# A float32 attention and mixer kernel: token transposes in halves, mixing products in pairs, loads on another queue, and five reorderings around them

## The chip, the cores and the metric

The kernel runs on one core of a Trainium2 chip. The metric is the device time of one execution in microseconds; lower is better.

## The reference

Inputs are `q`, `k`, `v` of 4 batches x 8 heads x 576 positions x 64, a small network `w1`, `b1`, `w2` (hidden width 32) that makes a position bias, and the mixer's weights, which are float64.

```python
scores = q @ k.T / 8
x = log1p(|i - j|) / log1p(max(i, 1))              # 576 x 576
bias = relu(x[..., None] @ w1 + b1) @ w2           # one 576 x 576 table per head
out = softmax(scores + bias) @ v                   # per batch and head
x = out, heads side by side                        # 4 x 576 x 512
u = x + transpose(transpose(x) @ U @ V)            # mixing over positions, U 576 x 32
result = u + relu(u @ w_ch1) @ w_ch2               # 512 -> 2048 -> 512
```

## The kernel before

It has four stretches.

**The network** (0 to 68 us) makes the bias of all heads in 36 tables. For each table one hidden block comes from ScalarE and three from VectorE (`bias_hid`, lines 308 and 310), TensorE multiplies them (`bias_mm`, line 317), ScalarE brings the result into one of eight `ring` slots (`bias_out`, line 332), and two DMAs on SyncE's queue (four for each of the first four tables, line 342) carry it into its place in the bias (line 338). The ten hidden slots let VectorE run about two tables ahead. Meanwhile the first pair of heads does a part of its work (`first(...)`: `Sn` is a scores block on TensorE, `Tn` adds the bias on VectorE, `En` is the exponential on ScalarE). Six DMAs, `pair_loads(1)`, fetch pair 1's q and k; they are issued at tables 9 to 14 of the loop.

Every DMA of the program counts its completion on one of eight semaphores, which are taken in turn in program order over all the queues. An issue on any queue waits until the transfer that had its semaphore before, eight DMAs earlier in program order, has landed.

**Attention** (76 to 300 us) runs over 16 pairs of heads, 9 slots each, in an order written out by hand (`SLOTS`: engines take their instructions in this order; one prime is the pair before, two primes the one before that). `R0` and `PM` divide the rows left over from 4 x 128 (`norm_m`, line 417, on GpSimd) and `I0` transposes them; `X` are other transposes, `AV` the product with v, `A` and `D` bring the output back into token order in `x_sb`. `Q1` to `Q4` split the next pair's q and k into a high and a low float32r part on GpSimd. From pair 2 on the float64 weights of group 0 are converted beside (`VA`, `VD`, `VS`, `VJ`: ScalarE, VectorE, GpSimd).

**Mixing** comes once for each batch, three times in the pair behind a batch and once at the end: `MT` to `MX` build the product with U, `H0` to `H4` multiply by V, one 128-row block each (`mix_h`), `HD` adds x (`mix_add`, line 594), `U` stores to DRAM (`mix_store`).

**The channel network** (from about 290 us) takes 18 blocks of 128 tokens: `make_ut` transposes a block (line 717), splits it into high and low parts, `mlp1` (line 756) and `mlp2` (line 779) multiply. It runs 36 steps, 4 groups of weights by 9 blocks of 256 tokens. The weights of group 1 are converted while steps 3 to 8 run: `background(n)` takes the next n small groups of conversion instructions after each part of a step. All PSUM tiles share four buffers; a new tile takes the buffer that was released longest ago.

Of the kernel before, what the change touches and what calls it, by code (L numbers as in the profile page):

```python
# [20 lines left out]
DM = H * D  # L21
# [4 lines left out]
P = 128  # L26
# [15 lines left out]
CW = 256  # L42

SLOTS = (
    "S0 E7' X10' MF' AV1'' T0 E8' MS' N8'' I1' VS1' C10' MX' E0 CO1'' M' VJ1' CI1' N0 CM' H3' "
    "VP0' R0",
    "S1 HD3' U3' T1 VA0",
    "S2 T2 X20' H4' Q1 VP1' Q2 C20' HD4' U4' LA",
    "S3 T3 PM H1' H0' X30' Q3",
    "S4 C30' HD1' U1' H2' HD0' U0' E3 T4 E2 HD2' U2' R8''",  # L50
    "S5",
    "S6 VD0 T5 E1 A0'' AV0' E4 VS0 A1'' VA1 T6 Q4 LB D0'' VJ0 I0 X00 D1'' CO0' CI0 E6",
    "S7 MT VD1 C00",
# [12 lines left out]
def kernel(  # L66
# [75 lines left out]
    qk_ops, raws = {}, {}  # L142
    v_t = {}

    def pair_loads(p):

        b, hp = divmod(p, HP)

        src = qk[b, hp]

        def part(i, lo, to, n):
            if (p, i) not in raws:
                raws[p, i] = rawp.tile([P, (QQ, KA + KB)[i]], F32, tag=f"raw{i}", name="raw")
            return raws[p, i][lo : lo + D, to : to + n]

        def q(lo):
            nc.sync.dma_start(
                out=part(0, lo, 0, QQ).rearrange("d (t n) -> d t n", t=2),
                in_=src[:, 0 : 2 * (S + LEFT)].rearrange("d (t n) -> d t n", t=2)[:, :, 0:S],
            )  # L160

        def k(lo, to, n, a):
            nc.sync.dma_start(out=part(1, lo, to, n), in_=src[:, a : a + n])

        return [
            lambda: q(0),
            lambda: q(D),
            lambda: k(0, 0, KA, K0),
            lambda: k(D, 0, KA, K0 + KA),
            lambda: k(0, KA, KB, K0 + S),  # L170
            lambda: k(D, KA, KB, 2 * K0 - KB),
        ]
# [10 lines left out]
    def prep_ops(p, early=False):  # L183


        hi = qkp.tile([P, 2 * KD * TB], F32R, tag="hi", name="hi")
        lo = qkp.tile([P, QKW], F32R, tag="lo", name="lo")
        qk_ops[p] = (hi, lo)

        parts = [(raws[p, 0], hi[:, 0:QQ], lo[:, 0:QQ]), (raws[p, 1], hi[:, QQ:QKW], lo[:, QQ:QKW])]  # L190

        def high(raw, h, l):
            nc.gpsimd.tensor_scalar(out=h, in0=raw, scalar1=1.0, scalar2=0.0, op0=ALU.mult, op1=ALU.add)

        def low(raw, h, l):
            eng = nc.vector if early else nc.gpsimd
            eng.tensor_tensor(out=l, in0=raw, in1=h.bitcast(F32), op=ALU.subtract)  # L197

        return [lambda o=o, i=i: o(*parts[i]) for i in range(2) for o in (high, low)]

# [337 lines left out]
            )  # L538

    mixt = {}  # L540
    stages = cycle([(tabp, "tab"), (tabp, "extra"), (mix, "y"), (mix, "th"), (mix, "tl")])

    def mix_t():
        t = psum("mt")[:, 0, :]
# [18 lines left out]
        mixt["t"] = t  # L563

    def mix_hi():
        mixt["h"] = mix.tile([P, DM], F32R, tag="th", name="th")
        nc.scalar.copy(out=mixt["h"], in_=mixt["t"])

    def mix_lo():
        mixt["l"] = mix.tile([P, DM], F32R, tag="tl", name="tl")  # L570
        nc.vector.tensor_tensor(out=mixt["l"], in0=mixt["t"], in1=mixt["h"].bitcast(F32), op=ALU.subtract)

    def mix_fold():
# [9 lines left out]
        o = mixt["q"][D:P]  # L583
        nc.vector.tensor_tensor(out=o, in0=mixt["s"][D:P], in1=o.bitcast(F32), op=ALU.subtract)

    def mix_h(c):
        mixt[c] = psum("mh")[:, 0, :]
        mm(mixt[c], lhsT=vq[:, c * P : (c + 1) * P], rhs=mixt["q"], start=True, stop=True)  # L588

    def mix_add(c):  # L590
        n = P if c < 4 else LEFT
        pool, tag = next(stages)
        y = mixt["y", c] = pool.tile([P, DM], F32, tag=tag, name="y")
        nc.vector.tensor_tensor(out=y[0:n], in0=mixt[c][0:n], in1=x_sb[0:n, c, :], op=ALU.add)

    def mix_store(b, c):
        n = P if c < 4 else LEFT
        nc.sync.dma_start(out=u_dram[b * S + c * P : b * S + c * P + n, :], in_=mixt["y", c][0:n])

    NP = B * HP  # L600

# [110 lines left out]
        nc.sync.dma_start(out=acc[i], in_=u_dram[i * P : (i + 1) * P, :])  # L712

    def make_ut(j, i):
        bank = psum("tu")[:, 0, :].rearrange("p (k q) -> p k q", k=KD)
        for k in range(KD):
            nc.tensor.transpose(bank[:, k, :], acc[j * TT + i][:, k * P : (k + 1) * P], ident)  # L717
        sl = slice(i * P, (i + 1) * P)
        nc.scalar.copy(out=uth[j][:, :, sl], in_=bank)  # L719
        if j == SPLIT:  # L720
            parts = [(at[:, :, i, :], k, k + n) for at, k, n in utl[j]]
        else:
            parts = [(utl[j][:, :, sl], 0, KD)]
        for dst, a, e in parts:
            nc.vector.tensor_tensor(  # L725
                out=dst, in0=bank[:, a:e], in1=uth[j][:, a:e, sl].bitcast(F32), op=ALU.subtract
            )

    def split(g, which, k, a, e):
        def fin(y):  # L730
            h, l = (w[k][:, a:e] for w in wq[g][2 * which : 2 * which + 2])
            nc.scalar.copy(out=h, in_=y)
            nc.gpsimd.tensor_tensor(out=l, in0=y, in1=h.bitcast(F32), op=ALU.subtract)

        return fin
# [140 lines left out]
    order = [32, 33, 34, 35] + [8 * c + i for c in range(4) for i in (0, 4, 1, 5, 2, 6, 3, 7)]  # L876
    early = {11: 0, 19: 1, 21: 2, 28: 3, 30: 4, 36: 5, 37: 6}
    preps[-1] = prep_ops(0, True)
    second = pair_loads(1)
    for i in range(len(order) + 3):  # L880
        if i == 2:
            nc.vector.tensor_scalar(
                out=table[:, CUT:NTAB], in0=table[:, CUT:NTAB], scalar1=w1_sb, scalar2=None, op0=ALU.mult
            )
        if 2 <= i < len(order) + 2:
            bias_mm(order[i - 2])
        if i < len(order):
            bias_hid(order[i])
        if i == 1:
            nc.vector.reciprocal(out=g8_sb, in_=ps)  # L890
        if 2 <= i < len(order) + 2:
            bias_out(order[i - 2])
        if i == 22:
            preps[0] = prep_ops(1, True)
        if 5 <= i < 9 or i in (22, 23, 25, 26):
            preps[-1 if i < 9 else 0].pop(0)()
        if 9 <= i < 15:
            second.pop(0)()
        if i - 1 in early:
            first(f"E{early[i - 1]}")  # L900
        if i - 1 == 11:
            first("N0")
        if i in early:
            first(f"S{early[i]}", f"T{early[i]}")
    done.update((f"Q{i}", 0) for i in range(1, 5))
    constants()
    x_sb = mix.tile([P, 5, DM], F32, tag="x_sb", name="x_sb")
    vq = mix.tile([P, 640], F32R, tag="vq", name="vq")
    nc.gpsimd.memset(x_sb[D:P, 4, :], 0.0)

    jobs = [(u32, 160, fin_u)]
    jobs += [(v4[:, a : min(a + CW, 640)], min(CW, 640 - a), fin_v(a, min(a + CW, 640))) for a in range(0, 640, CW)]
# [21 lines left out]
    for p in range(NP):  # L934
        if p > 0:
            new_pair(p)
        for s in range(9):
            if s == 3:
                load_v(p)
            if p == CONV_FROM - 1 and s in (0, 2, 4):  # L940
                conv["jobs"][s // 2][0]()
            period(p, s)
            if p == NP - 3 and s == 1:
                wq[0] = early_weights(0)
                feed = chain(first_weights(0), first_weights(1))
            if p == NP - 2 and s == 1:
                wq[0] += early_weights(1)
            if p == NP - 1 and s == 1:
                for i in range(9):
                    acc[i] = bias3[:, i * DM : (i + 1) * DM]  # L950
            if (p, s) in FEED:
                next(feed, None)
            if p == NP - 1 and s in (1, 2, 3):
                load_acc(2 * s - 2)
                load_acc(2 * s - 1)

    def run(*steps):
        for o in steps:
            o()

    m = [mlp1(n) for n in range(3)]
    y = [mlp2(n) for n in range(2)]
    def last_mix(c):
        mix_h(c)
        mix_add(c)
        mix_store(B - 1, c)

    def ut_in(t):
        return t[:, LINE : LINE + UT].rearrange("p (k f) -> p k f", k=KD)
# [38 lines left out]
    mix_fold()  # L1008
    mix_sum()
    mix_rest()  # L1010
    for i, c in enumerate((4, 0, 1, 2, 3)):
        run((m[2][1:] + y[1])[i])
        last_mix(c)
        if i > 2:
            make_ut(3, i - 3)
    p1.close()

    def pool(name, bufs):
# [13 lines left out]
    for n in range(2, NG * NB + 1):  # L1032
        g, j = divmod(n, NB)
        if n == 2:
            t = w3p.tile([P, LINE + 4 * WQ - 2 * DM], F32R, tag="w", name="wq")
            w = [t[:, LINE + i * DM : LINE + (i + 1) * DM] for i in range(4 * KD - 2)] + spare
            wq[1] = [w[i : i + KD] for i in range(0, 4 * KD, KD)]
        elif j == 0 and g + 1 < NG:
            wq[g + 1] = wq[g - 1]
        if g + 1 < NG and (n == 2 or (j == 0 and g > 0)):  # L1040
            queue += pipeline(weight_jobs(g + 1, split))
            queue[1:1] = [[]] * (8 if n > 2 else 0)
        steps = mlp1(n) if 2 < n < NG * NB else []
        if 2 < n < NB - 1:
            feed = [lambda i=i: make_ut(n + 1, i) for i in range(TT)]
            steps = steps + feed if n == 3 else feed + steps
        if n > 2:
            steps += mlp2(n - 1)
        for i, o in enumerate(steps):
            o()  # L1050
            background(2 if n >= NB or i == 0 else 1)


# [68 lines left out]
```

## Time and profile before

| | us |
|---|---|
| median of 3 runs | 725.97 (724.94 to 728.79) |
| the profiled execution | 726.99 |
| its span in the trace | 725.1 |
| TensorE busy (matmul) | 692.3, 95% of the span |
| VectorE / ScalarE / GpSimd busy | 446.5 / 354.6 / 216.8 |

The profiled execution is 1.0 us above the median. TensorE is busy in 95% of the span, so what is read below is where it is not, where it runs at its lower clock, and what it spends between matmuls.

### The profile page before, as it was taken

The page shows a single profiled execution, that of the slowest core. Times are in us where ns is not written, and L with a number is a line of the kernel's source. Part 1 is how long each engine was busy: PE and PEld are TensorE (multiplying, and loading weights), DVE is VectorE, ACT ScalarE, POOL GpSimd, SP SyncE. Part 2 cuts the span into 40 slices and gives each one's busy share as a digit, 9 for nine tenths or more (in the row PEclk, how much of TensorE's full clock was granted, in tenths as well). Part 3 has the DMA queues.
Part 4 walks back from the last instruction along what each step waited for, and adds up shares of the span by engine and source line. Part 5 has one row for each costly group of instructions (what it writes and reads, how often), then busy time and mean ns, then how long its engine had stood idle before and what let it go on. Part 6 is the DMA issues. An engine that isn't in the chain of part 4 may idle for free.

```text
span 725.1 us, 16712 instructions
## 1 busy us (share of the span) xinstructions
PE 692.3 (95%) x6708; PEld 575.9 (79%) x6708; DVE 446.5 (62%) x929; ACT 354.6 (49%) x763; POOL 216.8 (30%) x234
## 2 busy tenths in 40 slices
PE   6987799999999999999799999999999999999998
PEld 4554677667767867868689899898898998988986
DVE  7997589999999886434567548812288522122122
ACT  6887699879989889511444233410135201101000
POOL 1000457755755744100243325600056300000000
PEclk9999799999999999999899999999999999999999
DMA  4767734564565365104321212300022000010111
GB/s 127 185 197 215 186 84 110 143 200 141 154 178 172 99 179 180 44 1 148 136 71 62 59 40 77 102 15 1 1 77 96 18 1 1 1 59 31 57 54 63
DMA packets 39885, 68.25 MB, mean 94 GB/s; under 512 B 5888, under 2 KB 12544, under 8 KB 39808
## 3 DMA queue, kind: packets, MB, share of 16 engines
q1 hardware_dynamic: 39424, 67.01, 31.9%
q8 instruction: 53, 0.87, 0.5%
q14 instruction: 24, 0.20, 0.1%
q10 hardware_dynamic: 384, 0.18, 0.1%
HBM read 45.02 MB, written 11.53 MB: 78 GB/s over the span
## 4 chain that ended last, share of the span: by engine, by line
PE 85%; DVE 5%; ACT 3%; DMA 3%; issue 2%; SPq 1%; POOL 0%; DVEq 0%; ACTq 0%; POOLq 0%
PE po L779 28%; PE ph L756 27%; PE o L498 10%; PE sc L366 9%; PE tb L440 4%; PE bs L317 2%; DVE ring L310 2%; DMA bias<-ring 1%; PE mh L588 1%; ACT p L399 1%; PE tx L440 1%; PE ti L440 1%; DMA wraw<-in_w_ch_dram 1%; PE tu L717 1%; DVE wt L220 1%
## 5 line engine op out<-in xcount | busy, mean ns | idle before, releaser
L761 ACT ACTIVATE hh<-ph 128x1024 fp32r<-128x1024 f32 x36 | 36.9, 1025 | 190.5 <-PE ph L756 190.4
L762 DVE SCALAR_TENSOR_TENSOR hh<-ph,hh 128x1024 fp32r<-128x1024 f32 x36 | 44.1, 1225 | 130.6 <-ACT hh L761 130.6
L236 POOL TENSOR_TENSOR wy<-wt,wy 128x256 int32<-128x256 int32 (+1 forms) x68 | 52.5, 772 | 218.5 <-DVE wt L231 189.5
L779 PE MATMUL po<-bias,hh 128*128 128x512 f32 x432 | 105.0, 398 | 3.7 <-DVE hh L762 3.7
L399 ACT ACTIVATE p<-p,st 128x576 f32<-128x576 f32 x128 | 98.3, 772 | 3.9 <-DVE st L381 3.8
L381 DVE CUSTOM_DVE_ANT_0 p<-sc,bias 128x576 f32<-128x576 f32 x128 | 92.8, 751 | 8.7 <-PE sc L366 5.4
L779 PE MATMUL po<-wq,hh 128*128 128x512 f32 x360 | 98.1, 394 | 0.0
L779 PEld LDWEIGHTS po<-bias,hh 128*128 128x128 f32 x432 | 81.3, 192 | 20.7 <-DVE hh L762 4.2
L498 PE MATMUL o<-pt,v 128*64 128x320 f32 (+1 forms) x640 | 84.7, 411 | 0.1
L779 PEld LDWEIGHTS po<-wq,hh 128*128 128x128 f32 x360 | 66.5, 188 | 14.3
L756 PE MATMUL ph<-ut,bias 128*128 128x256 f32 x512 | 66.9, 279 | 0.3 <-DVE ut L725 0.3
L498 PEld LDWEIGHTS o<-pt,v 128*64 128x64 f32 x640 | 43.1, 136 | 28.9 <-DVE st L381 1.3
L756 PE MATMUL ph<-ut,wq 128*128 128x256 f32 x512 | 65.0, 276 | 0.0
L756 PEld LDWEIGHTS ph<-ut,bias 128*128 128x128 f32 x512 | 63.0, 188 | 1.0 <-DVE ut L725 0.5
L756 PEld LDWEIGHTS ph<-ut,wq 128*128 128x128 f32 x512 | 62.0, 188 | 1.0
L197 POOL TENSOR_TENSOR lo<-raw,hi 128x1152 fp32r<-128x1152 f32 (+1 forms) x28 | 59.4, 2122 | 1.7
L366 PE MATMUL sc<-hi 64*128 64x288 f32 (+1 forms) x320 | 56.7, 346 | 2.0 <-DVE x_sb L527 0.6
L423 ACT COPY pt<-tb 128x1024 f32<-128x1024 f32 x48 | 47.8, 1014 | 17.8 <-PE tb L440 9.4
L317 PE MATMUL bs<-ring,small_sb 128*32 128x64 f32 (+2 forms) x780 | 51.1, 355 | 5.3 <-DVE ring L310 2.4
L782 DVE TENSOR_TENSOR acc<-po,acc 128x512 f32<-128x512 f32 x36 | 24.9, 692 | 49.8 <-PE po L779 49.7
L756 PE MATMUL ph<-bias 128*128 128x256 f32 x352 | 48.5, 282 | 0.7 <-ACT bias L719 0.7
L366 PE MATMUL sc<-lo,hi 64*128 64x288 f32 (+1 forms) x320 | 48.8, 295 | 0.0
(106 smaller groups left out, 1219.8 us busy)
## 6 DMA issues: line engine op xcount, KB each, us to landing
wraw<-in_w_ch_dram SPq DMA_DIRECT2D x64, 256.0 KB
raw<-in_qk_dram SPq DMA_DIRECT2D x32, 288.0 KB
bias<-ring SPq DMA_DIRECT2D x64, 144.0 KB
v<-in_vp_dram SPq DMA_DIRECT2D x16, 320.0 KB
u_dram<-y SPq DMA_DIRECT2D x16, 256.0 KB
raw<-in_qk_dram SPq DMA_DIRECT2D x32, 88.0 KB
raw<-in_qk_dram SPq DMA_DIRECT2D x32, 72.0 KB
bias<-u_dram SPq DMA_DIRECT2D x9, 256.0 KB
```

Of the source, the lines that this page charges most:

```text
L197: eng.tensor_tensor(out=l, in0=raw, in1=h.bitcast(F32), op=ALU.subtract)
L236: nc.gpsimd.tensor_tensor(out=st["y"], in0=st["t"], in1=st["y"], op=ALU.add)
L317: mm(bs[T][32 * cg : 32 * cg + 32, a, o : o + n], lhsT=w2_sb, rhs=hids[T][cg][:, i : i + n], start=True, stop=True, tile_position=(0, 32 * ...
L366: mm(ps[0:n, a, 0:HALF], lhsT=q[r, q0 : q0 + n], rhs=k[r, k0 : k0 + HALF], start=(i == 0), stop=(i == len(terms) - 1),)
L381: nc.vector.tensor_tensor_reduce(out=halves(dst), in0=d.pop(("ps", s))[:, :, 0:HALF], in1=halves(bias_at(p % HP, s)), scale=-0.125, scalar ...
L399: nc.scalar.activation(out=dst, in_=dst, func=AF.Exp, bias=st[:, s : s + 1], scale=-1.0, accum_out=st[:, 10 + s : 11 + s])
L423: nc.scalar.copy(out=out, in_=in_)
L440: nc.tensor.transpose(bank[:, h, i * D : (i + 1) * D], src[r, a : a + P], ident[r, r])
L498: mm(o[hd * D : (hd + 1) * D, 0:n], lhsT=v[:, vb * D : (vb + 1) * D], rhs=pt[:, pb, :], start=(j == 0), stop=(j == 4),)
L756: mm(d, lhsT=w, rhs=u, start=(i == 0), stop=(i == 3 * KD - 1))
L762: nc.vector.scalar_tensor_tensor(out=hl[n], in0=st["ps"], scalar=0.0, in1=hh[n].bitcast(F32), op0=ALU.max, op1=ALU.subtract)
L779: mm(ps, lhsT=h, rhs=w, start=(m == 0), stop=(m == 3 * FG - 1))
```

## The change

1. `make_ut` transposes a block by `flip`, as attention does: for each 128 columns two transposes of 64 rows, into two banks, and the copies read both banks.
2. Mixing's five products go into three PSUM tiles (two, two, one), with one add and one store for each; the slots of `H`, `HD`, `U` are moved.
3. `pair_loads(1)` is issued on ScalarE's queue instead of SyncE's.
4. `R0` and `PM` of pair 0 stand right behind the network's loop, and the clearing of a part of `x_sb` on GpSimd, which stood ahead of them, moves to the beginning of pair 1.
5. The low part of q is made in three pieces, that of k in two (`prep_ops`, from pair 2 on).
6. The high part of group 0's second weights is copied by VectorE instead of ScalarE (`split`).
7. After the last mixing, the two `make_ut(3, .)` come ahead of the two parts of `mlp2(1)`, and mixing's products ahead of both.
8. The conversion of group 1's weights gets seven empty groups behind its first loads, and takes two groups at every fourth part of a step.

```diff
@@ SLOTS
-    "S0 E7' X10' MF' AV1'' T0 E8' MS' N8'' I1' VS1' C10' MX' E0 CO1'' M' VJ1' CI1' N0 CM' H3' "
+    "S0 E7' X10' MF' AV1'' T0 E8' MS' N8'' I1' VS1' C10' MX' E0 CO1'' M' VJ1' CI1' N0 CM' H0' "
     "VP0' R0",
-    "S1 HD3' U3' T1 VA0",
-    "S2 T2 X20' H4' Q1 VP1' Q2 C20' HD4' U4' LA",
-    "S3 T3 PM H1' H0' X30' Q3",
-    "S4 C30' HD1' U1' H2' HD0' U0' E3 T4 E2 HD2' U2' R8''",
+    "S1 HD0' U0' T1 VA0",
+    "S2 T2 X20' H1' Q1 VP1' Q2 C20' HD1' U1' LA",
+    "S3 T3 PM H2' X30' Q3",
+    "S4 C30' HD2' U2' E3 T4 E2 R8''",
@@ prep_ops
         def low(raw, h, l):
-            eng = nc.vector if early else nc.gpsimd
-            eng.tensor_tensor(out=l, in0=raw, in1=h.bitcast(F32), op=ALU.subtract)
+            eng, n = (nc.vector, 1) if early else (nc.gpsimd, 3 if raw is parts[0][0] else 2)
+            w = l.shape[1] // n
+            for a in range(0, n * w, w):
+                eng.tensor_tensor(
+                    out=l[:, a : a + w], in0=raw[:, a : a + w], in1=h[:, a : a + w].bitcast(F32), op=ALU.subtract
+                )
@@ mixing
-    def mix_h(c):
-        mixt[c] = psum("mh")[:, 0, :]
-        mm(mixt[c], lhsT=vq[:, c * P : (c + 1) * P], rhs=mixt["q"], start=True, stop=True)
+    def mix_h(g):
+        mixt[g] = psum("mh")
+        for i in range(stages[g][2]):
+            c = 2 * g + i
+            mm(mixt[g][:, i, :], lhsT=vq[:, c * P : (c + 1) * P], rhs=mixt["q"], start=True, stop=True)
@@ make_ut
-        bank = psum("tu")[:, 0, :].rearrange("p (k q) -> p k q", k=KD)
+        ps = psum("tu")
         for k in range(KD):
-            nc.tensor.transpose(bank[:, k, :], acc[j * TT + i][:, k * P : (k + 1) * P], ident)
+            flip(ps, k, acc[j * TT + i], k * P)
+        bank = ps[:, :, 0 : KD * D].rearrange("p h (k q) -> p h k q", k=KD)
@@ split
-            nc.scalar.copy(out=h, in_=y)
+            copy("d" if (g, which) == (0, 1) else "a", h, y)
@@ the network and the first pair
-    second = pair_loads(1)
+    second = pair_loads(1, nc.scalar)
...
+    first("R0", "PM")
     done.update((f"Q{i}", 0) for i in range(1, 5))
     constants()
...
-    nc.gpsimd.memset(x_sb[D:P, 4, :], 0.0)
...
+        if p == 1:
+            nc.gpsimd.memset(x_sb[D:P, 4, :], 0.0)
@@ the last mixing
-    for i, c in enumerate((4, 0, 1, 2, 3)):
-        run((m[2][1:] + y[1])[i])
-        last_mix(c)
-        if i > 2:
-            make_ut(3, i - 3)
+    for g in range(3):
+        run(m[2][1 + g])
+        last_mix(g)
+    for i in range(TT):
+        make_ut(3, i)
+        run(y[1][i])
@@ the channel network's loop
-            queue[1:1] = [[]] * (8 if n > 2 else 0)
+            queue[1:1] = [[]] * (8 if n > 2 else 7)
...
-            background(2 if n >= NB or i == 0 else 1)
+            background(2 if n >= NB or i % 4 == 0 else 1)
```

## Rows read from the trace of the kernel before

**Rows 1.** Part 4 of the page: the chain that ended last, by engine.
```profile
PE 85%; DVE 5%; ACT 3%; DMA 3%; issue 2%; SPq 1%; POOL 0%; DVEq 0%; ACTq 0%; POOLq 0%
```

**Rows 2.** Stretches of 20 us: busy us of each engine, granted clock, DMA share, GB/s.
```profile
core 0: us, PE busy (x) PEld busy (x) DVE busy (x) ACT busy (x) POOL busy (x), PEclk, DMA share, GB/s
60.00:80.00 20.00, 11.42 (x172) 9.07 (x174) 9.44 (x26) 10.19 (x18) 2.50 (x4) 0.76 0.86 231
120.00:140.00 20.00, 18.63 (x282) 14.57 (x284) 19.21 (x47) 17.95 (x45) 15.33 (x16) 1.00 0.43 111
340.00:360.00 20.00, 16.27 (x96) 14.20 (x95) 8.33 (x16) 6.45 (x15) 2.93 (x4) 0.83 0.53 182
```

**Rows 3.** Timeline, 56 to 82 us: start, us, engine, line, instruction, [idle before].
```profile
67.02 0.80 ACT L332 ACTIVATE ring<-bs,g 128x640 f32<-128x640 f32 x1 [1.05 <-PE bs L317]
...
68.78 0.16 DVE L409 RECIPROCAL st<-st 128x1 f32<-128x1 f32 x1
...
74.48 0.52 POOL L909 MEMSET x_sb<- 64x512 f32 x1 [32.23 <-DMA bias<-ring]
...
76.20 0.37 PE L440 MATMUL ti<-ident,pm 64*128 64x64 f32 x2 [8.58 <-POOL pm L417]
...
78.30 0.76 DVE L381 CUSTOM_DVE_ANT_0 p<-sc,bias 128x576 f32<-128x576 f32 x1 [0.84 <-PE sc L366]
```

**Rows 4.** The chain in order of time, 20 to 75 us: start, us, what.
```profile
25.14 2.78 DMA bias<-ring
...
34.42 4.49 DMA bias<-ring
...
71.27 3.07 DMA bias<-ring
```

**Rows 5.** Timeline of SyncE's queue, from 21 us.
```profile
21.27 5.04 SPq L338 DMA_DIRECT2D bias<-ring  x8
```

**Rows 6.** Waits of SyncE's queue: us in total, times, longest.
```profile
SPq L163 <- DMA bias<-ring: 0.7, 1, 0.7
```

**Rows 7.** Timeline of ScalarE, around 20 us.
```profile
20.44 0.79 ACT L332 ACTIVATE ring<-bs,g 128x640 f32<-128x640 f32 x1 [0.91 <-PE bs L317]
```

**Rows 8.** Timeline of VectorE, around 39 us.
```profile
39.17 0.76 DVE L381 CUSTOM_DVE_ANT_0 p<-sc,bias 128x576 f32<-128x576 f32 x1 [1.79 <-DMA raw<-in_qk_dram]
```

**Rows 9.** Timeline of GpSimd, 121 to 132 us.
```profile
123.26 2.67 POOL L197 TENSOR_TENSOR lo<-raw,hi 128x1152 fp32r<-128x1152 f32 x1
```

**Rows 10.** Line 220 (`VD`): ns min/median/max, first and last start, forms.
```profile
L220 DVE SCALAR_TENSOR_TENSOR wt<-wt,eps x68: 293/420/2125, 98.3 to 568.6; 128x256 f32<-128x256 f32 x66, 128x160 f32<-128x160 f32 x1, 128x128 f32<-128x128 f32 x1
```

**Rows 11.** Groups by line and form: busy us, mean ns, idle before.
```profile
L594 DVE TENSOR_TENSOR y<-mh,x_sb 128x512 f32<-128x512 f32 x16 | 10.6, 679 | 1.0 <-PE mh L588 1.0
```

**Rows 12.** The chain in order of time, 299 to 304 us.
```profile
299.50 0.44 PE tu L717 x4
299.94 1.42 PE ph L756 x12
301.36 0.64 PE tb L440 x16
302.00 1.61 PE ph L756 x12
```

**Rows 13.** Timeline, 284 us.
```profile
284.37 0.40 PE L440 MATMUL tx<-ident,ot 64*128 64x64 f32 x6 [0.88 <-ACT pt L423]
```

**Rows 14.** Timeline, 338 us.
```profile
338.13 0.38 PE L756 MATMUL ph<-bias 128*128 128x256 f32 x1 [0.68 <-ACT bias L719]
```

**Rows 15.** Timeline of ScalarE, 349 us.
```profile
348.94 0.43 ACT L213 ACTIVATE wt<-wraw 128x256 f32<-128x256 f32 x1 [10.86 <-DMA wraw<-in_w_ch_dram]
```

**Rows 16.** The chain in order of time, 343 to 370 us.
```profile
343.08 5.83 DMA wraw<-in_w_ch_dram
...
352.05 5.42 PE po L779 x12
...
364.00 5.47 PE po L779 x24
369.47 0.87 PE tu L717 x8
```

More of the change, by code (lines that the diff above doesn't have):

```diff
@@ L143, with pair_loads @@
     v_t = {}
-    def pair_loads(p):
+    def pair_loads(p, eng=nc.sync):
         b, hp = divmod(p, HP)
@@ L156, in q @@
         def q(lo):
-            nc.sync.dma_start(
+            eng.dma_start(
                 out=part(0, lo, 0, QQ).rearrange("d (t n) -> d t n", t=2),
@@ L162, in k @@
         def k(lo, to, n, a):
-            nc.sync.dma_start(out=part(1, lo, to, n), in_=src[:, a : a + n])
+            eng.dma_start(out=part(1, lo, to, n), in_=src[:, a : a + n])
         return [
@@ L540 @@
     mixt = {}
-    stages = cycle([(tabp, "tab"), (tabp, "extra"), (mix, "y"), (mix, "th"), (mix, "tl")])
+    stages = ((tabp, "tab", 2), (mix, "tt", 2), (tabp, "extra", 1))
     def mix_t():
@@ L565, in mix_hi @@
     def mix_hi():
-        mixt["h"] = mix.tile([P, DM], F32R, tag="th", name="th")
+        tt = mix.tile([P, 2, DM], F32R, tag="tt", name="tt")
+        mixt["h"], mixt["l"] = tt[:, 0, :], tt[:, 1, :]
         nc.scalar.copy(out=mixt["h"], in_=mixt["t"])
     def mix_lo():
-        mixt["l"] = mix.tile([P, DM], F32R, tag="tl", name="tl")
         nc.vector.tensor_tensor(out=mixt["l"], in0=mixt["t"], in1=mixt["h"].bitcast(F32), op=ALU.subtract)
@@ L584, in mix_rest, with mix_add, mix_store @@
         nc.vector.tensor_tensor(out=o, in0=mixt["s"][D:P], in1=o.bitcast(F32), op=ALU.subtract)
-    def mix_h(c):
-        mixt[c] = psum("mh")[:, 0, :]
-        mm(mixt[c], lhsT=vq[:, c * P : (c + 1) * P], rhs=mixt["q"], start=True, stop=True)
[L590 to L598, printed above, removed]
+    def mix_h(g):
[3 more added lines that the diff above has]
+            mm(mixt[g][:, i, :], lhsT=vq[:, c * P : (c + 1) * P], rhs=mixt["q"], start=True, stop=True)
+    def mix_add(g):
+        pool, tag, k = stages[g]
+        n = P if g < 2 else LEFT
+        y = mixt["y", g] = pool.tile([P, k, DM], F32, tag=tag, name="y")[0:n]
+        nc.vector.tensor_tensor(
+            out=y, in0=mixt[g][0:n, 0:k, :], in1=x_sb[0:n, 2 * g : 2 * g + k, :], op=ALU.add
+        )
+    def mix_store(b, g):
+        y = mixt["y", g]
+        r = b * S + 2 * g * P
+        n = P if g < 2 else LEFT
+        k = stages[g][2]
+        nc.sync.dma_start(out=u_dram[r : r + k * n, :].rearrange("(c p) d -> p c d", p=n), in_=y)
     NP = B * HP
@@ L714, in make_ut, with halves_of @@
     def make_ut(j, i):
-        bank = psum("tu")[:, 0, :].rearrange("p (k q) -> p k q", k=KD)
+        ps = psum("tu")
         for k in range(KD):
-            nc.tensor.transpose(bank[:, k, :], acc[j * TT + i][:, k * P : (k + 1) * P], ident)
+            flip(ps, k, acc[j * TT + i], k * P)
+        bank = ps[:, :, 0 : KD * D].rearrange("p h (k q) -> p h k q", k=KD)
+        def halves_of(t):
+            return t.rearrange("p k (h q) -> p h k q", h=2)
         sl = slice(i * P, (i + 1) * P)
-        nc.scalar.copy(out=uth[j][:, :, sl], in_=bank)
+        nc.scalar.copy(out=halves_of(uth[j][:, :, sl]), in_=bank)
         if j == SPLIT:
@@ L725, in make_ut @@
             nc.vector.tensor_tensor(
-                out=dst, in0=bank[:, a:e], in1=uth[j][:, a:e, sl].bitcast(F32), op=ALU.subtract
+                out=halves_of(dst), in0=bank[:, :, a:e], in1=halves_of(uth[j][:, a:e, sl]).bitcast(F32),
+                op=ALU.subtract,
             )
@@ L962, with last_mix @@
     y = [mlp2(n) for n in range(2)]
[L963 to L966, printed above, removed]
+    def last_mix(g):
+        mix_h(g)
+        mix_add(g)
+        mix_store(B - 1, g)
     def ut_in(t):
```

## The prediction

> **What bounds the kernel.** I read the page first, then the stretches, then the timeline where a stretch falls short. The chain that ended last runs over TensorE for 85% of the span [rows 1], so a part of the change is worth what it takes off TensorE's stalls, its half-clock time or its own work; elsewhere it is worth nothing. Three stretches fall short [rows 2]. In 60 to 80 us TensorE is busy 11.42 of 20 at a granted clock of 0.76: behind the network it waits for the divided leftover rows. In 120 to 140 it is busy 18.63 while VectorE is at 19.21: there VectorE is the tight engine. In 340 to 360 it is busy 16.27 at a clock of 0.83: a stall inside the channel network. From about 360 us on there are no gaps to win.
>
> **The change part by part.** The sum is made against the profiled execution, 726.99, which is 1.0 above the median of the runs shown.
>
> *Leftover norm and pair 1's loads (parts 3 and 4).* The last table leaves ScalarE at 67.02 + 0.80 = 67.8. The reciprocal is there at 68.9, but GpSimd stands before the clearing of `x_sb` until the last bias transfer has landed, and TensorE starts at 76.20 after 8.58 idle [rows 3]. Behind the network at once, the division needs what lies between the end of the clearing (75.00) and 76.20, which is 1.2 us: TensorE could go on near 70.2. What is late next is `T7` at 78.30 [rows 3], which needs the bias itself: the last transfer, issued at 71.27, lands 3.07 later, at 74.34 [rows 4]. With the loads where they were, T7 would come at 74.4, a gain of 3.9.
>
> The loads then move this landing both ways. Off SyncE, they save six issues at 5.04 / 8 = 0.63 [rows 5], 3.8 us: the last table's second transfer would be issued at 67.8 + 0.63, not at 71.27, and land 2.8 earlier; VectorE's 1.79 wait at 39.17 [rows 8], for the first quarter of the bias, whose transfer took 4.49 [rows 4], would go too. That is 4.6 more, 8.5 in all. But on ScalarE each load now waits in that engine's own order for the landing of the transfer eight DMAs before, which sits on SyncE's queue; such a wait on unrelated data is in the trace [rows 6]. Queued behind it on ScalarE are the next table's hidden block and evacuation, and for these wait TensorE, then VectorE (through the hidden slots), then SyncE. The first load follows the evacuation that ends at 20.44 + 0.79 = 21.2 [rows 7]. Its semaphore was last taken by the transfer issued at 21.27, the first of eight [rows 5], which by a neighbour lands 2.78 later [rows 4], at 24.0. So ScalarE is held 2.8, and it pays six issues, 3.8: 6.6. It had 0.91 idle of its own there [rows 7], and I let the hidden slots take another 1 (an estimate): VectorE is some 4.8 late, less the 1.79 that disappears, so the network ends 3.0 later, at 70.8. SyncE is then no longer behind: the last issue comes at 71.4 and lands at 74.5. T7 comes at about 74.6, where the leftover path arrives too (70.8 + 0.3 for the reciprocal, 1.2, and the 2.1 from 76.20 to 78.30, which lay at half clock). I take -3.7. Bounds: -8.5 without any hold; +2.8 if the later loads are held as well, which I bound by one full round of eight transfers, 5.04 of issues and a landing of 4.49, less 3 of work meanwhile: 6.5 later. The issues moved from SyncE pass no other queue; the clearing, moved behind, holds only GpSimd's work of pair 1, which waits for pair 0's scores anyway.
>
> [...]
>
> *Low parts in pieces (5).* The same subtraction and a little more start-up on GpSimd, which is idle a quarter of the time even in 120 to 140 [rows 2]. But one low part holds GpSimd 2.67 [rows 9], and the conversion's step on VectorE, 0.42 in the median, took up to 2.125 [rows 10]; I take GpSimd's instruction for the cause. With pieces of some 0.9 the hold is at most 0.9, about 1.2 less. It counts only where VectorE is tight: two pairs near 120 to 150, there once each, -1.5 after some slack. Bounds 0 and -3.4 (two holds of 1.7 each gone).
>
> *Mixing in pairs (2).* Five adds of 0.679 [rows 11] become three; two adds in one cost VectorE between 0.68 and 1.36. TensorE does the same five products with fewer changes of its tiling. Hidden behind TensorE mostly: -0.3, bounds -1.4 and +0.5 (a double add ahead of `T1`, not covered, in some pairs).
>
> *Copies on VectorE (6).* ScalarE's copy queue holds TensorE 0.88 at 284 us [rows 13]; two of the four moved copies stand there. The cost on VectorE is not in the trace; 0.679 for an add of this size [rows 11] bounds it from above, nothing from below. -0.8, bounds -0.9 and +0.5.
>
> *Transposes by halves (1).* A block's four transposes take 0.44 on the chain, two blocks 0.87 [rows 12, 16]. Attention's sixteen half transposes, as many as two blocks will need, take 0.64 among full-height products, and the twelve products behind them 1.61 instead of 1.42 [rows 12]: 0.83 together. Two blocks in a row, five times, gain 0.04 each. One block alone, six times, needs eight halves: between 0.32 and 0.64, plus 0.19, against 0.44, so +0.07 to +0.39. The first two blocks stand among half transposes and save some 0.4. Sum 0, bounds -1 and +2.
>
> [...]
>
> *Last mixing (7).* TensorE stands 0.68 before `mlp1(3)` [rows 14], for ScalarE's copy of block 3; VectorE's subtraction of about 0.68 [rows 11] comes behind it. With `mlp2(1)` after each transpose, 2.7 us of products cover both. -1.2, bounds -0.5 and -1.6.
>
> *Conversion later (8).* In step 3 ScalarE stands 10.86 us in front of the first conversion, until the weights land at 348.9 [rows 15, 16]. Queued behind it is the evacuation of `mlp1(3)`, so its PSUM buffer is released late and the second part of `mlp2(2)` cannot start. [...] With seven empty groups the first conversion comes behind the first part of `mlp2(2)` in program order, and so behind the evacuation. Late next would be the end of the conversion: 51 groups and 7 make 58, and the parts of steps 3 to 8 take 46 and 12, which is 58, so the last one is issued just before step 9. -6.4, bounds -6.7 and -3.7 (the clock falls anyway).
>
> Sum: -3.7 - 1.5 - 0.3 - 0.8 + 0 - 1.2 - 6.4 = -13.9, so 713.1 for such an execution and 712 for the median.
>
> **The rivals.**
> - *The holds on ScalarE eat the first gain.* Rows 6 and the 4.49 landing speak for it, the hidden slots against it: the network ends 6.7 later instead of 3.0, the first term is 0, and the time is 716.
> - *No hold:* SyncE's relief counts in full, -8.5 instead of -3.7: 707.5. The order of semaphores speaks against it.
> - *The stall at 345 us stays in part,* because the weights still land late or the PSUM buffer waits for something else: 3 of the 6.4 lost, 715 to 718.5. The eager issue of the loads, unchanged, speaks against it.
> - *Slower: the loads and the bias transfers feed each other.* If each of the six loads is held for a full round (4.49 landing plus eight issues of 0.63, 9.5 us, less ScalarE's own work in the 2.7 tables that eight DMAs span, 2.7 x (2 x 0.79 + 0.63) = 5.9), 3.6 each, the network ends 22 later. It decides from 3.0 + 13.9 = 17 later, 2.8 a load: then the time is above 726, at the full price 731. SyncE catching up meanwhile speaks against it.
>
> **How the numbers follow.** Forecast 0.52, holds eat the gain 0.17, no hold 0.18, stall stays 0.08, loop 0.05. The time is that of the forecast. The range leaves the loop and the ends of the others out: downward 712 - 4.8 - 3 for the low bounds of the pieces and the copies, 704; upward 716 and another 4 for terms that give nothing, 720. A difference of 0.5%, 3.6 us, is about what a measurement of this kernel can tell from no change. All cases but the loop lie beyond it on the fast side, with the fringe of the stalled ones inside: faster 0.91, same 0.05, slower 0.04.
>
> **What would show it.** Right: TensorE's idle time behind the network falls from 8.58 to under 4, T7 near 74.6; ScalarE stands about 2.8 before the first load near 21 us and the network ends near 71; no L220 over 1.3 us; no gap at 345 and the clock at 1.0 in 340 to 360; `make_ut` costs as before. Wrong: the network ends near 66 (no hold) or beyond 74; a gap before step 9; the idle time behind the network taken over by a wait for the bias.

## The result and the profile after

The changed kernel takes 717.99 us (median of 4 runs, 717.14 to 718.49) against 726.07 for the kernel before in the same runs: ratio 0.9882, 95% interval 0.9853 to 0.9911. The forecast was 712.0 within 704 to 720. The range held, but 8.1 us came where about 14 were forecast, and the parts of the sum did not all come as forecast. The profiled execution is 718.49 (span 716.4). All medians here are over the fast executions; one slow one of 1685.72 us, in experiment 6, is left out.

The stretches of the kernel after, columns as in [rows 2]:

```profile
20.00:40.00 20.00, 13.56 (x218) 9.31 (x210) 12.53 (x28) 12.05 (x19) 1.88 (x2) 0.83 0.51 140
60.00:80.00 20.00, 16.11 (x281) 11.94 (x272) 14.28 (x37) 14.70 (x25) 1.04 (x2) 1.00 0.72 200
80.00:100.00 20.00, 16.02 (x226) 13.12 (x228) 13.62 (x36) 15.41 (x39) 13.12 (x16) 0.83 0.62 161
120.00:140.00 20.00, 18.94 (x294) 14.75 (x291) 18.63 (x50) 18.86 (x50) 15.08 (x19) 1.00 0.49 131
340.00:360.00 20.00, 20.00 (x150) 17.70 (x149) 12.50 (x20) 7.83 (x17) 4.81 (x6) 1.00 0.35 116
```

Two of the three weak stretches of [rows 2] are better: 340 to 360 has no gap and the full clock, 120 to 140 is busier (60 to 80 cannot be compared: the network ends later in it, and the wait behind the network now lies in 80 to 100, where TensorE is busy 16.02 at a clock of 0.83). A new weak stretch has appeared at 20 to 40, where TensorE is busy 13.56 at a granted clock of 0.83 while the DMA engines are at 0.51 (0.81 in experiment 1, where TensorE is busy 18.36): not a shortage of bandwidth. SyncE's queue tells what happened, first by its waits (us in total, times, longest), then in the chain in order of time:

```profile
SPq L346 <- DMA raw<-in_qk_dram: 8.7, 1, 8.7
SPq L342 <- DMA raw<-in_qk_dram: 3.4, 2, 2.3
```
```profile
21.86 4.11 DMA raw<-in_qk_dram
...
25.99 0.59 SPq L346
...
29.29 2.40 DMA bias<-ring
...
31.91 0.16 DVE praw L385
```

SyncE, which carries the bias, stands 8.7 us, from 17.3 to 26.0, in front of a transfer of a table made long before (such a wait of a queue is called a stand below). It waits for a load of pair 1 that ScalarE issues only at 21.86 and that lands at 25.97. The bias transfers behind it are late, and with them `T0` on VectorE. TensorE waits behind that (timeline of the kernel after):

```profile
31.91 0.76 DVE L385 CUSTOM_DVE_ANT_0 praw<-sc,bias 128x576 f32<-128x576 f32 x1 [6.89 <-DMA bias<-ring]
33.16 0.42 PE L321 MATMUL bs<-extra,small_sb 128*32 128x64 f32 x2 [6.01 <-DVE extra L314]
```

So the network ends later. The end of the network, against [rows 3]:

```profile
72.87 0.80 ACT L336 ACTIVATE ring<-bs,g 128x640 f32<-128x640 f32 x1 [1.04 <-PE bs L321]
...
75.53 0.28 PE L444 MATMUL ti<-ident,pm 64*128 64x64 f32 x2 [2.06 <-POOL pm L421]
...
81.83 0.76 DVE L385 CUSTOM_DVE_ANT_0 p<-sc,bias 128x576 f32<-128x576 f32 x1 [5.14 <-DMA bias<-ring]
82.60 0.52 POOL L955 MEMSET x_sb<- 64x512 f32 x1 [7.12 <-DMA raw<-in_qk_dram]
82.64 0.78 ACT L403 ACTIVATE p<-p,st 128x576 f32<-128x576 f32 x1 [5.23 <-DVE st L385]
82.65 0.18 PEld L444 LDWEIGHTS ti<-ident,p 64*128 64x128 f32 x2 [4.35 <-DVE st L385]
82.66 0.37 PE L444 MATMUL ti<-ident,p 64*128 64x64 f32 x2 [4.21 <-DVE st L385]
```

The last evacuation ends at 73.67, not 67.82. The early leftover norm does what it should, 2.06 us of idle time instead of 8.58, but `T7` comes at 81.83 instead of 78.30, and TensorE idles 4.21 for it. The first product with v starts at 89.78 instead of 86.0: the start lost 3.8 us. From there to the last matmul the kernel after takes 623.05 and the kernel before 635.48, 12.4 less. Two places of it, VectorE's conversion step against [rows 10], and blocks in the channel network against [rows 12, 16]:

```profile
L224 DVE SCALAR_TENSOR_TENSOR wt<-wt,eps x68: 412/426/989, 102.1 to 560.0; 128x256 f32<-128x256 f32 x66, 128x160 f32<-128x160 f32 x1, 128x128 f32<-128x128 f32 x1
```
```profile
342.90 0.64 PE tu L444 x16
343.54 5.65 PE po L796 x24
349.19 0.64 PE tu L444 x16
349.83 5.64 PE ph L773 x48
```

No conversion step takes 2.1 us any more, and `mlp2(2)` runs its 24 products in one piece at the full clock.

### The profile page after: what moved, and what is told of

Same layout as the page of the kernel before. It is cut to its first block, busy times and chain, and to the rows that moved or that the text cites. A ratio compares the mean times of both kernels' runs of the same rounds, so it can differ in the third digit from the quotient of the medians.

```text
span 716.4 us, 16875 instructions
## 1 busy us (share of the span) xinstructions
PE 687.0 (96%) x6780; PEld 573.2 (80%) x6780; DVE 443.1 (62%) x925; ACT 351.8 (49%) x759; POOL 224.7 (31%) x276
## 4 chain that ended last, share of the span: by engine, by line
PE 88%; DMA 3%; DVE 3%; ACT 2%; issue 2%; POOL 1%; SPq 1%; DVEq 0%; ACTq 0%; POOLq 0%
PE ph L773 28%; PE po L796 28%; PE o L502 11%; PE sc L370 8%; PE tb L444 4%; PE bs L321 3%; DMA bias<-ring 2%; DVE ring L314 2%; PE tx L444 1%; PE mh L594 1%; PE ti L444 1%; ACT p L403 1%; PE tu L444 1%; DMA raw<-in_qk_dram 1%; PE mt L550 1%
## 5 line engine op out<-in xcount | busy, mean ns | idle before, releaser
L796 PE MATMUL po<-bias,hh 128*128 128x512 f32 x432 | 102.3, 392 | 0.0
L796 PEld LDWEIGHTS po<-bias,hh 128*128 128x128 f32 x432 | 79.7, 188 | 16.2
L199 POOL TENSOR_TENSOR lo<-raw,hi 128x384 fp32r<-128x384 f32 (+1 forms) x70 | 67.5, 991 | 1.7
L321 PE MATMUL bs<-ring,small_sb 128*32 128x256 f32 (+2 forms) x780 | 52.1, 361 | 4.1 <-DVE ring L314 1.5
L799 DVE TENSOR_TENSOR acc<-po,acc 128x512 f32<-128x512 f32 x36 | 24.9, 691 | 46.6 <-PE po L796 46.6
```

The source lines that it names most:

```text
L199: eng.tensor_tensor(out=l[:, a : a + w], in0=raw[:, a : a + w], in1=h[:, a : a + w].bitcast(F32), op=ALU.subtract)
L321: mm(bs[T][32 * cg : 32 * cg + 32, a, o : o + n], lhsT=w2_sb, rhs=hids[T][cg][:, i : i + n], start=True, stop=True, tile_position=(0, 32 * ...
L796: mm(ps, lhsT=h, rhs=w, start=(m == 0), stop=(m == 3 * FG - 1))
```

## The experiments

Where an effect is small, the stretch from the first product with v to the last matmul (623.05 in the kernel after) is given beside the median: it leaves out the start, whose length differs from one execution to the next (with the early norm `T7` waits for the first of the last table's two bias transfers, by the semaphores in its wait, and starts 2.9 to 5.5 us after that one's issue in these traces). Behind the start the traces repeat well: of the four runs that edit nothing but the loads three have 623.13 to 623.15, and the fourth, on GpSimd's queue, has 623.92 and loses the difference in the first 26 us.

**1. Loads back on SyncE.**

```diff
-    second = pair_loads(1, nc.scalar)
+    second = pair_loads(1)
```

> The changed kernel with pair 1's loads issued on SyncE again; the other seven parts stay. Theory A (the loads on ScalarE's queue hold completion semaphores that SyncE's bias transfers need, so SyncE stands 8.7 us from 17.3 to 26.0): the stand is gone, the network ends near 67.8 as before, T7 starts near 74.4 instead of 81.8, and the time is 7.5 under the changed kernel's 718, so 710 to 711. Rival B (the early leftover norm and the moved clearing cost the start its 3.8 us): the network still ends near 73.7 or T7 still comes near 82, and the time stays at 717 to 719. Rival C (two queues contend for the DMA engines): as A here, told apart by the loads on GpSimd's queue.

712.51 us (712.18 to 712.89), ratio to the kernel before 0.9827 (0.9793 to 0.9861). The stretch at 20 to 40 recovers:

```profile
20.00:40.00 20.00, 18.36 (x319) 9.96 (x311) 18.23 (x41) 17.42 (x27) 1.40 (x1) 1.00 0.81 186
```

The network ends at 67.50, as the theory had it, and rival B is out. `T7` comes at 75.94, not 74.4, so 5.5 us of the expected 7.5 came.

**2. The loads alone, on the kernel before.**

```diff
-    def pair_loads(p):
+    def pair_loads(p, eng=nc.sync):
...
-    second = pair_loads(1)
+    second = pair_loads(1, nc.scalar)
```

> The kernel before with the loads on ScalarE's queue and nothing else of the change. Theory A: the same stand of about 8.7 us on SyncE, the network ends 5.9 later, near 73.7, the leftover rows' path behind it shifts by as much or a little more, and the time is 6 to 6.5 over before, 732. Rival B: no change beyond 1 us. My forecast's own mechanism (ScalarE held by its loads, the network 3.0 later, less what SyncE saves): the last bias transfer at 71.4 instead of 71.3, so 726.

731.65 us, ratio 1.0092 (1.0056 to 1.0128): 6.2 slower. The network ends at 72.94 and the same wait stands on SyncE's queue:

```profile
SPq L342 <- DMA raw<-in_qk_dram: 8.7, 1, 8.7
```

The part makes the kernel slower by itself, and my forecast's mechanism (no change) is refuted.

**3. The leftover norm alone, on the kernel before.**

```diff
+    first("R0", "PM")
     done.update((f"Q{i}", 0) for i in range(1, 5))
...
-    nc.gpsimd.memset(x_sb[D:P, 4, :], 0.0)
...
+        if p == 1:
+            nc.gpsimd.memset(x_sb[D:P, 4, :], 0.0)
```

> The kernel before with only the leftover norm right behind the network and the clearing of x_sb moved to pair 1. Theory A: TensorE's idle time behind the network falls from 8.6 to 2 to 3 us, T7 then waits for the last bias transfer and starts near 74.4 instead of 78.3: 3.9 under before, 722. Rival B: T7 comes no earlier than 78, time 726 or more.

722.86 us (720.34 to 724.83), ratio 0.9968 (0.9947 to 0.9989): between 0.8 and 3.8 faster. In its trace TensorE idles 2.07 in front of the leftover rows and `T7` starts at 71.90, earlier than the expected 74.4: the transfer that it needs was issued at 68.82 and landed at 71.74 (in the kernel before 70.68 and 73.86). This trace is of a quick execution, 720.89, 2.0 under the median.

**4. The loads on GpSimd's queue.**

```diff
-    second = pair_loads(1, nc.scalar)
+    second = pair_loads(1, nc.gpsimd)
```

> The changed kernel with the six loads issued on GpSimd's queue, whose transfers count on semaphores of their own, so that the bias transfers on SyncE take the eight in turn as if there were no loads. The same bytes move on two queues. Theory A: no stand on SyncE, six issues of 0.63 fewer there (3.8 us), the network ends between 63 and 67.8, T7 near 70, and the time is 704 to 708, under the kernel with the loads back on SyncE. Rival C (two queues contend): the bias transfers land late as in the changed kernel, network end near 73, time 716 to 718.

710.23 us (708.61 to 714.27), ratio 0.9814 (0.9762 to 0.9866). SyncE waits for no load in the network, and the network ends at 67.66. Two queues move the same bytes as in the kernel after, so contention (rival C) is not what cost it 3.8 us. But the end of the network is no earlier than with the loads on SyncE, though six issues are saved there. From 40 to 60 us VectorE is busy all of the time (third column of busy times), and before that it lost what the relief gave:

```profile
20.00:40.00 20.00, 17.31 (x296) 11.72 (x291) 17.25 (x39) 16.15 (x25) 4.68 (x6) 1.00 0.92 216
40.00:60.00 20.00, 19.00 (x322) 12.49 (x318) 20.00 (x47) 19.39 (x33) 0.00 (x0) 1.00 0.73 207
```
```profile
28.02 0.76 DVE L385 CUSTOM_DVE_ANT_0 praw<-sc,bias 128x576 f32<-128x576 f32 x1 [2.75 <-PE bs L321]
```

`T1` no longer has the wait of 1.62 that it has at 38.86 in experiment 1, but `T0` waits 2.75. The row names TensorE, whose scores were done by 24.9; the last of the sixteen transfers that `T0` needs, issued at 20.68, lands at 27.81 (at 22.25 in experiment 1), with the loads in flight beside it and the DMA engines at 0.92. So the two queues seem to get in each other's way here, at a lower price than the stand's; that is read from these times and was not isolated by a run. At the end, only the last bias transfer is issued sooner, at 69.18 instead of 70.98. This version and that of experiment 1 are both faster than either kernel; their intervals overlap.

**5. Loads on ScalarE, five tables later.**

```diff
-        if 9 <= i < 15:
+        if 14 <= i < 20:
             second.pop(0)()
```

> The changed kernel with pair 1's loads still on ScalarE's queue, but at tables 14 to 19 of the loop instead of 9 to 14. Theory A (SyncE stands until a load that holds its semaphore has been issued by ScalarE and has landed): the first load now comes behind the evacuation of the table that ends near 31 us, lands near 34.5, and the bias transfer that is given its semaphore, of a table made near 25 us, waits for it: no stand at 17 us, but one of some 6 to 7 us that begins near 28. The network ends near 72, time 716 to 719. Rival (the stand came from the first transfers' own slow landing near 17 us): it stays at 17, or goes with the loads' contention, and there is none at 28.

A single run, 711.57 us, so without an interval. The stand moved as the theory had it: none at 17, but one that ends at 31.8, when the first load (issued at 28.15) has landed. SyncE's waits and the stretch:

```profile
SPq L342 <- DMA raw<-in_qk_dram: 6.1, 3, 5.0
```
```profile
20.00:40.00 20.00, 18.14 (x316) 9.68 (x309) 17.05 (x37) 16.37 (x25) 1.15 (x1) 1.00 0.61 175
```

The price was wrong: the network ends at 69.72, 2.2 late instead of 4.5, and the time is 4 to 7 us below what I expected. The transfers that `T0` needs were through before this stand began, so VectorE did not wait in front of `T0`, and TensorE kept its clock in 20 to 40. `T1` waits 3.58 at 40.78 instead, and the clock is 0.91 in 40 to 60. So this stand of 5.0 cost the network's end 2.2 and that of 8.7 in the kernel after 6.2: both times the price was nearer to the wait of the next scores block, 3.58 and 6.89, than to the stand.

**6. Loads on SyncE, five tables later.** Both edits, of experiments 1 and 5.

> The changed kernel with pair 1's loads on SyncE's queue again, at tables 14 to 19 of the loop. With the loads on SyncE at tables 9 to 14, VectorE waits 1.6 us at 38.9 for a bias transfer that is queued behind loads, and the last bias transfer is issued 3.5 behind the end of the network. Theory (only the order on SyncE's queue counts, and the bias transfers of the tables that the next scores block needs now come first): no stand at 17 or at 28, the wait at 38.9 gone, the network ends 1 to 1.6 earlier than 67.5, time 711 (710 to 712.5). Rival (SyncE has the same 86 issues and stays behind by as much at the end): network end and time as with the loads at tables 9 to 14, 712.5.

712.84 us (710.85 to 713.63), ratio 0.9819 (0.9792 to 0.9846), as with the loads on SyncE at their old place. The wait at 38.9 is gone, but VectorE now waits 1.05 and 1.35 at 44 and 51 for the high parts of the late loads, the network ends at 67.27, and the last bias transfer is issued at 72.94. The rival is right about the time.

**7. Low parts whole again.**

```diff
-            eng, n = (nc.vector, 1) if early else (nc.gpsimd, 3 if raw is parts[0][0] else 2)
+            eng, n = (nc.vector, 1) if early else (nc.gpsimd, 1)
```

> The changed kernel with each low part on GpSimd in one instruction again. Theory A (while GpSimd works through one low part, VectorE's conversion step beside it is held): its longest instance goes back from 0.99 to over 2 us, the first part of attention, from the first product with v to the eleventh, takes 72.2 us again instead of 69.5, and the time is 2.5 to 3 over the changed kernel's 718, so 720.5 to 721. Rival B (those 2.7 us come from mixing's products in pairs or from copies moved to VectorE): the long instances come back or not, but the time stays within 0.7 of 718.

721.67 us, ratio 0.9954 (0.9934 to 0.9973). From the first product with v to the last matmul it takes 626.54, 3.5 more. GpSimd's low part and the conversion step behind it (timelines of GpSimd and VectorE):

```profile
127.14 2.66 POOL L199 TENSOR_TENSOR lo<-raw,hi 128x1152 fp32r<-128x1152 f32 x1
```
```profile
127.98 2.10 DVE L224 SCALAR_TENSOR_TENSOR wt<-wt,eps 128x256 f32<-128x256 f32 x1
```

The step on VectorE, 0.42 in the median, ends 0.28 behind the end of GpSimd's instruction at 129.80. Why it is held so long no run shows. The first part of attention (to the eleventh block of products with v) grew from 69.5 to 72.2, as expected; the rest was lost behind it. In that first part two steps are long again, 2.10 and 1.50, together 2.8 more than 0.42 each.

**8. Conversion at its old place.**

```diff
-            queue[1:1] = [[]] * (8 if n > 2 else 7)
+            queue[1:1] = [[]] * (8 if n > 2 else 0)
...
-            background(2 if n >= NB or i % 4 == 0 else 1)
+            background(2 if n >= NB or i == 0 else 1)
```

> The changed kernel with the conversion of group 1's weights at its old place (no empty groups in front, two groups at the first part of a step only). Theory A: TensorE's gap near 345 and the half clock behind it come back, 6.4 in all, so 724 to 725. Rival B (the gap was closed by the earlier start of the loads or by the blocks in half transposes): no gap, 718.

719.22 us, ratio 0.9907 (0.9870 to 0.9943): not 724. The stretch takes 624.30, 1.3 more. TensorE's gap is 0.67, and the clock stays at 1.00:

```profile
347.74 3.04 PE L796 MATMUL po<-bias,hh 128*128 128x512 f32 x12 [0.67 <-DVE hh L779]
```

ScalarE still stands in front of the conversion, 9.11 us, but the weights are there at 344.6. Something else in the change brought them earlier (experiment 10).

**9. The last mixing as before.**

```diff
-    for g in range(3):
-        run(m[2][1 + g])
-        last_mix(g)
-    for i in range(TT):
-        make_ut(3, i)
-        run(y[1][i])
+    for i, g in enumerate((2, None, 0, None, 1)):
+        run((m[2][1:] + y[1])[i])
+        if g is not None:
+            last_mix(g)
+        if i > 2:
+            make_ut(3, i - 3)
```

> The changed kernel with the last mixing interleaved as before (three product tiles among the parts of mlp1(2) and mlp2(1), both blocks transposed behind). Theory A: the wait of 0.7 before mlp1(3) comes back and the blocks are no longer covered, 1.2 to 1.4 more, 719.3. Rival B: the gain came from the products in pairs there, so at most 0.4 more.

719.66 us, ratio 0.9925 (0.9896 to 0.9953); the stretch takes 624.51, 1.5 more. As forecast, but see the next one.

**10. Both, 8 and 9.**

> The changed kernel with both the last mixing and the conversion of group 1 at their old places. Undone singly, the trace of the conversion put back lost 1.3 us and that of the last mixing put back 1.5. Theory A (the two are two ways out of one stall: the stores of the last mixing hold SyncE's queue, so the weights land late, and the conversion that waits for them holds ScalarE; either edit alone ends most of it): undone together TensorE's gap of 3 to 4 us near 345 and the half clock behind it come back, about 7.9 in all, so 726. Rival B (two separate effects that add up): 2.9 in all, 721.

727.62 us (723.08 to 728.55), ratio to the kernel before 1.0021 (1.0000 to 1.0041). The stretch takes 631.82, 8.8 more than in the kernel after, where the two single ones add up to 2.7. Its gap, its clock, and SyncE's queue; under them the same queue in the kernel after:

```profile
353.18 5.15 PE L796 MATMUL po<-bias,hh 128*128 128x512 f32 x12 [4.58 <-DVE hh L779]
```
```profile
340.00:360.00 20.00, 15.42 (x108) 13.01 (x108) 7.48 (x14) 5.98 (x15) 2.92 (x4) 0.83 0.60 202
```
```profile
328.08 10.89 SPq L609 DMA_DIRECT2D u_dram<-y  x3
339.14 4.63 SPq L723 DMA_DIRECT2D acc<-u_dram  x9
343.87 12.43 SPq L210 DMA_DIRECT2D wraw<-in_w_ch_dram  x5
```
```profile
328.33 5.41 SPq L609 DMA_DIRECT2D u_dram<-y  x3
333.91 4.63 SPq L723 DMA_DIRECT2D acc<-u_dram  x9
338.64 13.53 SPq L210 DMA_DIRECT2D wraw<-in_w_ch_dram  x4
```

Theory A holds: undone together they cost 8.8, and TensorE's gap and the clock of 0.83 are back. The three stores of the last mixing stand on SyncE's queue ahead of the loads of the blocks and of the weights. With the mixing's products ahead they are through 5.2 us sooner, and the weights' loads start at 338.64 instead of 343.87. With the mixing alone put back (experiment 9) the loads start late too, at 343.72, but the conversion no longer stands in front of the evacuation, and TensorE has no gap in 340 to 360 and the full clock: either edit is a way out.

**11. Full-height transposes.**

```diff
         for k in range(KD):
-            flip(ps, k, acc[j * TT + i], k * P)
-        bank = ps[:, :, 0 : KD * D].rearrange("p h (k q) -> p h k q", k=KD)
+            nc.tensor.transpose(ps[:, 0, k * P : (k + 1) * P], acc[j * TT + i][:, k * P : (k + 1) * P], ident)
+        bank = ps[:, 0, :].rearrange("p (k h q) -> p h k q", k=KD, h=2)
```

> The changed kernel with make_ut's transposes 128 rows high again, into one bank. My forecast's sum of 0 for this part: blocks that stand in pairs gain or lose under 0.1 each, single blocks among the products 0.1 to 0.4 each, together within 1 us of 718. [...]

718.64 us, ratio 0.9904 (0.9868 to 0.9941); the stretch takes 622.99, 0.06 less. No difference, and the chain shows why:

```profile
349.28 0.87 PE tu L728 x8
350.15 5.45 PE ph L773 x48
```

Two blocks of full transposes and the 48 products behind take 0.87 + 5.45 = 6.32; in halves, in the fence of the result, 0.64 + 5.64 = 6.28. What the halves save (0.23) the products behind them lose (0.19).

**12. Copies back on ScalarE.**

```diff
-            copy("d" if (g, which) == (0, 1) else "a", h, y)
+            nc.scalar.copy(out=h, in_=y)
```

> The changed kernel with the copies of group 0's second weights on ScalarE again. My forecast's 0.8: TensorE's wait near 284 us comes back and the time is 718.8. Rival: ScalarE had room, VectorE pays as much as ScalarE saves, 718.

718.35 us, ratio 0.9897 (0.9867 to 0.9928), which the median alone cannot tell from the kernel after. The stretch takes 623.86, 0.8 more. The wait for it stands elsewhere than I had put it:

```profile
294.51 0.28 PE L444 MATMUL ti<-ident,p 64*128 64x64 f32 x2 [0.80 <-ACT p L403]
```

At 284 us TensorE waits 0.80 to 0.85 with the copies on either engine; the 0.80 in front of an exponential of ScalarE at 294.5 is what they cost there.

## Why the prediction was right or wrong

*Leftover norm and loads (-3.7 forecast, +3.8 measured, outside the bounds of -8.5 and +2.8): the step that failed.* The coupling was the right place to look, but I put the wait on the wrong queue. I had ScalarE held 2.8 before the first load; it issued that load at 20.58 without such a wait. It is SyncE that stands, 8.7. I had taken the eight semaphores as dealt in program order, so that a load shares its semaphore with bias transfers of its own time. In the trace of the kernel before it looks so: its 352 issues, four of them ScalarE's, count on eight semaphores, and 337 of the last 344 take that of the issue eight earlier in time. By the semaphores in the trace of the kernel after the second load, written behind nine tables, has the semaphore that SyncE's twelfth bias transfer, of the third table, takes next: the load is issued at 21.86 and lands at 25.97, the transfer is issued at 25.99. An early transfer thus waits for a load that ScalarE can reach only behind the evacuation of later tables. Experiments 1, 2, 4 and 5 show this: the stand comes with the loads alone, is gone on either other queue, and moves when the loads do. The cost of the stand is `T0`, 6.89 late. The relief of SyncE, 3.8 in my sum, did not move the network's end even without a stand (experiment 4): VectorE got back 1.62 at `T1` and lost 2.75 at `T0`. It brought the last bias transfer 1.8 forward. The norm by itself gave 0.8 to 3.8, against 3.9 forecast. One reading was off by 0.5: `T7` needs the last table's first transfer, which landed at 73.86 in the kernel before, and only `T8` the last one, at 74.35.

Of the rivals, *no hold* comes nearest to what GpSimd's queue shows: its first product with v starts at 78.74, 7.3 before the kernel before, against 8.5 worked out. But most of that is not SyncE's relief: in experiment 3, with the norm alone, it starts at 79.91, and part of both is the landing that differs between executions. On ScalarE's queue the loads alone made the kernel 6.2 slower (experiment 2). *The stall at 345 stays* holds the measured time in its 715 to 718.5, and *the holds eat the gain* is near it with 716, but neither has the mechanism. That the time fell within the range is in part luck: the start came out 7.5 worse than forecast, and the rest 2.2 better.

*Low parts (-1.5 forecast, -3.5 measured).* That VectorE's step is long beside a whole low part is shown (2.10 beside one of 2.66, at most 0.99 with the pieces), why it is, not; the size I gave it was too small. I counted two holds, and two it was, but I left a hold of 0.9 behind for the pieces and took off another 0.9 as slack; without the pieces they cost 2.7 to the eleventh block, near the 2.8 by which they are too long, and a further 0.8 behind it, where I had counted nothing. The bound was -3.4. The pieces cost GpSimd 0.7 us a pair: 4.24 whole (2.676 and 1.568), 4.96 in pieces (three of 1.029, two of 0.935).

*Last mixing and conversion (-1.2 and -6.4 forecast, -8.8 together).* The sum is near, the division was wrong. The 6.4 has two parts in the kernel before: 3.73 us without a product ahead of 352.05, then twelve products in 5.42 at a granted clock of 0.52 (352.0 to 357.5), 2.7 more than half of the 5.47 that twenty-four take from 364.00 at 1.00. No run shows that it is the idle time that lowers the clock, or what rate the lower clock is; the gap and the lower clock came and went together (a gap of 4.58 and 0.83 in 340 to 360 in experiment 10, 0.67 or none and 1.00 in experiments 8 and 9). They go with either edit, because the last mixing's place also moves its stores on SyncE's queue, and with them the weights' load. I followed its products and not its DMAs. The rival that the stall stays is refuted.

*Copies (-0.8 forecast, -0.8 in the trace)*, at another place than forecast. *Transposes by halves (0 forecast; in the trace they cost 0.06)*, with the terms as worked out: 0.04 for two blocks in a row. Sixteen halves take 0.64 where eight full ones take 0.87, and the 48 products behind them 5.64 instead of 5.45.

*Mixing in pairs (-0.3 forecast)* was not run alone. The parts measured behind the start, 3.5 + 8.8 + 0.8 - 0.1 = 13.0, exceed the 12.4 between the two kernels. If the parts add up, its own is within some 0.6 of nothing; that is not shown.

Of the signs I had named, no gap at 345, no long conversion step and the idle time under 4 came true; `T7` at 74.6 and the network's end at 71 did not, and "the idle time taken over by a wait for the bias" was the sign of error that appeared.

What stays open: why the transfer that `T7` needs lands 2.9 us after its issue in experiment 3 and 5.4 in experiment 1. By the semaphore events it counts sixteen completions: in experiment 3 they come between 71.51 and 71.74, in experiment 1 fifteen have come by 73.67 and the sixteenth comes at 75.78. One late part is worth 2.1 us there; what delays it is not shown.

## What to carry to other kernels

A DMA moved to another engine's queue can still be tied to the old queue through a shared completion semaphore, as these loads were (8.7 us of stand on SyncE): before moving one, look which transfer takes its semaphore next, and when the new engine can reach the issue. Of an edit that moves work, follow the DMAs too: here the stores of the last mixing, not its products, set when the weights' loads started, 338.64 or 343.87. Two edits against one stall are to be undone together before either is given its price.

## What the runs showed that I had not expected

The first of two stands of SyncE, 8.7 us, cost the network's end 6.2 (67.50 to 73.67) and the other, 5.0, cost 2.2; the scores block that came next waited 6.89 (`T0`) and 3.58 (`T1`, which waits 1.62 in experiment 1 too). Loads issued on GpSimd's queue counted on six semaphores of their own, so that what stands ahead of the prediction, that every DMA takes its turn on one of eight in program order, holds neither for that queue nor, as the stand shows, for the order. They left the bias transfers their turn, and yet the last one that `T0` needs landed 7.1 us after its issue beside them, against 2.4 in experiment 1.
